# Due times for ScalarE and VectorE work, and a last product in two column pieces

## The chip, the cores and the metric

The kernel runs on one core of a Trainium2 chip. Its time is what the device takes for one execution, in microseconds (us), and the median over several executions is compared. The engines are named as in the profile: PE (TensorE, matrix products), ACT (ScalarE), DVE (VectorE), POOL (GpSimd) and SP (SyncE). PE writes its results to PSUM, from where ACT and DVE read them. In this kernel POOL and SP mostly issue DMAs.

## What is computed

An attention without softmax feeds a two-layer network. There are 8 batches, 12 heads, 448 positions and a head size of 64; the network has width 768 and 2048 inner units, and runs over all 8 x 448 = 3584 rows.

```python
scores = scale * np.matmul(q, k.transpose(0, 1, 3, 2))   # scale = 1/sqrt(64)
attn = np.maximum(scores, 0.0) ** 2 / S                  # S = 448
attn_out = np.matmul(attn, v)
x = attn_out.transpose(0, 2, 1, 3).reshape(B * S, H * D) # 3584 x 768
h = x @ w_in                                             # 768 x 2048
g = 0.5 * h * (1.0 + erf(h / sqrt(2)))
out = g @ w_out                                          # 2048 x 768
```

## The kernel before, in words

**Stages of one batch.** The heads of a batch b are taken four at a time, in three groups g. For each group there are seven *score steps* i of 64 keys (`add_steps`, 539). A step is four matmuls into a PSUM tile `ps` (L552), then a relu with scaling into `a_sq`, either on ACT (L564) or on DVE (L566), then a square on DVE (L573). After the seven steps of a group comes the product *AV* (`add_av`, 600; L614) into a PSUM tile `pav`, and two copies of it into `xT`, one for each half, on DVE (L316) or ACT (L318). Then the first layer (`add_f1`, 650): sixteen products `psh` with the input weights, six matmuls each (L661), and after each a Gelu on ACT (L671) into the ring `h_sb`.

**The second layer.** It works on groups of two times 128 rows (`add_group`, 732). Each group is a matrix product by quarters with seven products of eight matmuls of 384 columns (L768) instead of eight, made from sums of inputs (`s_sb`, four *sums* on DVE, L749) and sums of weights (`t_sb`, made once, L706). The results leave PSUM by *passes* (`passed`): a copy (L316) or an addition (L802) on DVE into `p_sb` or the output tile `osb`. The last product of a group, `p3`, is added onto bank "c" after `c22` has read that bank, and its pass `c12` adds it to the right half of the group's first output tile. Then SP issues the stores (`store_rows`, L729). A store is split in two DMAs where the row order of the output asks for it. In the last group (g = 13) the store of that right half goes by the queues of ACT and SP, one DMA each. The first two blocks of rows are multiplied plainly (`add_plain`, L850).

**Buffers.** PSUM has three `w` tiles of two banks each, which `ps` and `pav` share, and two `f`-pool tiles of one bank, which `psh` and the products of the second layer take from the same pool. There are 14 `a_sq` tiles.

**Transposes.** For batch 0 and 1 PE transposes q and k. From batch 2 on, DVE reorders them into `pk` and `pq` (L395, L406), SP issues seven transposing DMAs into `kT` and `qT` (L498, L507), and POOL, behind a small copy `gate` (L519) that waits for the transposes, issues the loads of the batch after.

**What sets the order.** Everything is written as operations with the engines that may do them, an estimated duration, what they depend on, and which buffers they need and free (`Op`, 86). A planner (`Scheduler`, 100) places them in its own estimated time and so decides, while the program is built, on which engine and in which order each stands; the chip then runs each engine's queue in that order, and waits where a result or buffer is missing. The first 270 operations or so, up to about 57 us, have their engine and order written out in ORDER (68). After that PE follows a fixed list `pe_q`, which interleaves batch b's scores with the first layer of batch b - 1 and groups of the second layer. In each group g the list has two score steps, then the AV of the group before (or a product of the network where there is none), then two score steps, and later the other three. POOL has a fixed list as well. For ACT, DVE and SP, `pick` (131) takes among the next operations the one with the smallest estimated start plus a hand-set bias; the passes have -0.4 us, the sums -0.3, the Gelus -0.57. From batch 2 on, the relu of step i = 1 stands on DVE and all others on ACT (`DVE_STEPS`, 586). The estimates of the planner are no times of the chip.

Of the kernel before, what the change touches and what calls it, by code (L numbers as in the profile page):

```python
# [26 lines left out]
ND = DM // 2  # L27
# [13 lines left out]
ATT1_BIAS = 0.0  # L41
HALF_BIAS = -0.07
GELU_BIAS = -0.57
RELU_DVE = 0.3
DMA_FREE = 4.54
DMA_LAT = 2.13
SWITCH = 0.09
LEAD = 8
DVE_STEPS = (1,)
HALF_M = 6  # L50
PASS_BIAS = -0.4
SUM_BIAS = -0.3
TSUM_BIAS = 0.2
LEADS = {3: 8}
CARRY = 4


def cols(half):
# [9 lines left out]
ORDER = """  # L68
# [31 lines left out]
class Scheduler:  # L100
# [4 lines left out]
    WINDOW = 60  # L105

    def __init__(self, buffers):
        self.free = {"PE": 6.0, "ACT": 2.6, "DVE": 1.0, "POOL": 1.25, "SP": 0.9}
        self.bufs = {name: [0.0] * n for name, n in buffers.items()}
        self.open, self.mode, self.dma = [], None, DMA_FREE  # L110
        self.landed = [0.0] * 8
        self.log = []
    def add(self, engines, fn, deps=(), **kw):
        op = Op(engines, fn, deps, **kw)
        self.open.append(op)
        return op
# [11 lines left out]
            t = max(t, f)  # L128
        return t

    def pick(self, ops):
        top = None
        for n, op in enumerate(ops):
            t = self.ready(op)
            if t is None:
                continue
            for x, (eng, dur, lat) in enumerate(op.engines):
                est = max(t, self.free[eng])
                if isinstance(lat, tuple):
# [32 lines left out]
    def run(self, fixed):  # L172


        fixed = {e: list(v) for e, v in fixed.items()}
        inside = {id(o) for v in fixed.values() for o in v}

        names = {"P": "PE", "A": "ACT", "D": "DVE", "G": "POOL", "S": "SP"}
        gone = set()
        for word in ORDER.split():  # L180
            op, eng = self.open[int(word[1:])], names[word[0]]
            _, dur, lat = next(e for e in op.engines if e[0] == eng)
            self.commit(max(self.ready(op), self.free[eng]), op, eng, dur, lat)
            gone.add(id(op))
        fixed = {e: [o for o in v if id(o) not in gone] for e, v in fixed.items()}
        rest = [o for o in self.open if id(o) not in inside | gone]
        while rest or any(fixed.values()):
# [18 lines left out]
        self.open = []  # L206
        n = len(ORDER.split())
        for est, op, eng in self.log[:n] + sorted(self.log[n:], key=lambda x: x[0]):
            op.fn(eng)


@with_exitstack
def kernel(
# [325 lines left out]
    def add_steps(todo, bias=0.0, dve=False):  # L539
        for blocks in todo:  # L540
            box = {}
            w = S if blocks[0][3] is None else HS
            used = w * len(blocks)

            def fn_qk(e_, blocks=blocks, box=box, w=w):
                ps = box["ps"] = w_pp.tile([128, 2, NB], F32, tag="w", name="ps")
                for x, (b, g, i, half) in enumerate(blocks):
                    qT, kT = get_T(b)
                    for e in range(2):
                        r = slice(64 * e, 64 * e + 64)  # L550
                        for j in range(2):
                            nc.tensor.matmul(  # L552
                                ps[64 * j : 64 * j + 64, e, x * w : x * w + w],
                                kT[r, g, i * 128 + 64 * j : i * 128 + 64 * j + 64],
                                qT[r, 2 * g + j, cols(half)],
                                start=True,
                                stop=True,
                            )

            def fn_relu(e_, box=box, used=used):  # L560
                box["a2"] = apool.tile([128, 2, S], BF16, tag="a", name="a_sq")
                ar, ps = box["a2"][:, :, :used], box["ps"][:, :, :used]
                if e_ == "ACT":
                    A.activation(ar, ps, AF.Relu, scale=c_att)  # L564
                else:
                    V.tensor_scalar(  # L566
                        ar, ps, c_att, 0.0,
                        op0=mybir.AluOpType.mult, op1=mybir.AluOpType.max,
                    )
# [162 lines left out]
    def add_group(g):  # L732
# [30 lines left out]
        def product(bank, left, right, deps, need=(), frees=(), joint=()):  # L763
            def fn(e):
                if need:
                    box[bank] = f_pp.tile([128, NB], F32, tag="f", name="pso")
                for kf in range(K2):
                    nc.tensor.matmul(  # L768
                        box[bank][:, :ND],
                        left()[:, kf],  # L770
                        right[:, kf],
                        start=bool(need) and kf == 0,
                        stop=kf == K2 - 1,
                        skip_group_check=not need,
                    )

            d = K2 * (ND / 2400 + 0.0025)
            o = sch.add(
                (("PE", d, d + 0.24),), fn, deps, need=need, frees=frees, joint=joint, mode="F"
            )  # L780
# [13 lines left out]
                box["p"] = spool.tile([128, ND], F32, tag="p", name="p_sb")  # L794
            return box["p"]

        def passed(bank, out, other, deps, need=(), frees=(), joint=()):
            def fn(e):
                if other is None:
                    copy(e, out(), box[bank][:, :ND])  # L800
                else:
                    V.tensor_add(out(), box[bank][:, :ND], other())  # L802

            eng = e_copy(ND, 1)
# [19 lines left out]
        c22 = passed("c", part(1, right), part(1, right), [v3, p5])  # L824
        p4 = product("b", lambda: h(1, o2), tsum[4], [v3])
        c21 = passed("b", part(1, left), first, [p4, v3], frees=("f", "p"))
        p3 = product("c", lambda: box["s", 4], quad[1, 1], [c22, s4], frees=("s4",))
        c12 = passed("c", part(0, right), part(0, right), [p3], frees=("f",))
        if g < NG - 1:
            sch.add((("SP", 0.6, 2.8),), store(1, full, [nc.sync] * 2), [c22, c21], frees=("osb",))  # L830
            sch.add((("SP", 0.6, 2.8),), store(0, full, [nc.sync] * 2), [c11, c12], frees=("osb",))
# [6 lines left out]
        return [(1.3, o) for o in (p1, p6, p2, p7, p5, p4, p3)]  # L838

    plain = []  # L840

# [238 lines left out]
```

## Time and profile before

| | |
|---|---|
| median of 8 runs | 380.13 us |
| lowest and highest of them | 379.27 and 381.23 us |
| the profiled execution: its time | 379.27 us |
| its span, first to last instruction | 377.5 us |
| busy PE / DVE / ACT / POOL | 365.7 / 246.4 / 201.8 / 45.8 us |
| granted TensorE clock | 1.000 |
| relus on ACT (L564) / on DVE (L566) | 141 of 914 ns / 28 of 1088 ns on average |
| squares on DVE (L573) | 169 of 616 ns |
| DMA | 42.93 MB, 114 GB/s on average |

Lines such as L552 are lines of the kernel's file. In the timeline, each row has the start, the length, the engine with the line and operation, what is written from what, and how many instructions are merged in the row. A bracket at the end says how long the engine had been idle before, and what the work was waiting for. In the view of waits, each row has the engine and line that waited, what it waited for, the total in us, how often, and the longest. A matmul's own length is modelled and longer than its distance to the next one, so distances are read from the starts. "SPq" and "ACTq" rows are DMA issues on the queues of these engines.

### The profile page before, as it was taken

What the parts mean: (1) busy time and instruction counts of PE and PEld (TensorE: products, weight loads), DVE (VectorE), ACT (ScalarE), POOL (GpSimd) and SP (SyncE); (2) the same over time, 40 slices, a digit from 0 to 9 for tenths busy, and PEclk for the clock granted to TensorE, in tenths of its full rate; (3) what the DMA queues carried; (4) which work ended last, traced back from release to release, by engine and by line L of the source; (5) the groups of instructions that cost most, each with busy time, mean ns of one, the idle gap of its engine ahead of it and who ended that gap; (6) DMA issues with size and microseconds to landing.
All of it is one profiled execution on the core that took longest, in us unless ns stands there. A gap on an engine that the chain in (4) does not pass through costs nothing.

```text
span 377.5 us, 7915 instructions
## 1 busy us (share of the span) xinstructions
PE 365.7 (97%) x3333; PEld 201.5 (53%) x3333; DVE 246.4 (65%) x446; ACT 201.8 (53%) x307; POOL 45.8 (12%) x69
## 2 busy tenths in 40 slices
PE   8799999999999989999999999999999999999995
PEld 7576544455544555555555455555554555555663
DVE  3999981599944788843888458745884468601662
ACT  4998865875248635465346775566336762143000
POOL 8666402200020030002000200000000000000000
PEclk9999999999999999999999999999999999999999
DMA  9999999995779979649517590740203002200222
GB/s 172 196 201 205 200 188 112 203 203 107 127 147 177 146 112 224 148 93 159 104 42 158 96 197 2 173 58 3 82 3 85 0 2 84 67 18 2 83 85 83
DMA packets 69523, 42.93 MB, mean 114 GB/s; under 512 B 37744, under 2 KB 66032, under 8 KB 69488
## 3 DMA queue, kind: packets, MB, share of 16 engines
q0 software_dynamic: 30512, 22.47, 39.9%
q1 hardware_dynamic: 38656, 19.46, 24.3%
q8 instruction: 26, 0.43, 0.4%
q10 hardware_dynamic: 320, 0.51, 0.4%
q14 instruction: 9, 0.07, 0.1%
HBM read 45.61 MB, written 11.01 MB: 150 GB/s over the span
## 4 chain that ended last, share of the span: by engine, by line
PE 82%; DVE 7%; DMA 6%; ACT 1%; SPq 1%; POOL 1%; issue 1%; POOLq 0%
PE psh L661 34%; PE pso L768 32%; PE ps L552 8%; PE pav L614 6%; DMA wout_sb<-in_moe_w_out_dram 4%; DVE a_sq L573 2%; DVE a_sq L566 2%; DMA nk<-in_k_dram 1%; PE pso L850 1%; DVE s_sb L749 1%; SPq L507 1%; DVE osb L802 1%; DMA qT<-pq 1%; ACT a_sq L564 1%; DVE xT L316 1%
## 5 line engine op out<-in xcount | busy, mean ns | idle before, releaser
L661 PE MATMUL psh<-xT,win_sb 128*128 128x448 bf16 (+1 forms) x804 | 151.5, 344 | 0.1
L564 ACT ACTIVATE a_sq<-ps 128x896 bf16<-128x896 f32 (+1 forms) x141 | 123.2, 914 | 47.4 <-PE ps L552 47.2
L573 DVE TENSOR_TENSOR a_sq<-a_sq 128x896 bf16<-128x896 bf16 (+1 forms) x169 | 100.6, 616 | 41.8 <-ACT a_sq L564 41.6
L661 PEld LDWEIGHTS <-win_sb 128*128 128x128 bf16 x804 | 76.1, 98 | 71.4 <-issue 9.8
L671 ACT ACTIVATE h_sb<-psh 128x448 bf16<-128x448 f32 x128 | 70.0, 547 | 68.1 <-PE psh L661 56.2
L768 PEld LDWEIGHTS <-s_sb 128*128 128x128 bf16 x416 | 40.0, 98 | 28.3 <-issue 2.5
L552 PE MATMUL ps<-qT,kT 64*64 64x448 bf16 (+1 forms) x756 | 47.9, 336 | 4.6 <-DVE a_sq L566 1.8
L566 DVE TENSOR_SCALAR a_sq<-ps 128x896 bf16<-128x896 f32 x28 | 30.4, 1088 | 22.9 <-PE ps L552 22.5
L768 PEld LDWEIGHTS <-h_sb 128*128 128x128 bf16 x312 | 29.8, 98 | 22.1 <-issue 2.8
L768 PE MATMUL pso<-t_sb,s_sb 128*128 128x384 bf16 x208 | 38.1, 326 | 0.0
L768 PE MATMUL pso<-wout_sb,h_sb 128*128 128x384 bf16 x208 | 38.1, 326 | 0.0
L768 PE MATMUL pso<-wout_sb,s_sb 128*128 128x384 bf16 x208 | 38.0, 326 | 0.0
L614 PE MATMUL pav<-a_sq,v_sb 64*64 64x448 bf16 (+1 forms) x756 | 37.0, 330 | 0.8 <-ACT a_sq L564 0.4
L552 PEld LDWEIGHTS <-kT 64*64 64x64 bf16 x756 | 18.6, 105 | 27.5 <-issue 22.3
L802 DVE TENSOR_TENSOR osb<-pso,p_sb 128x384 f32<-128x384 f32 x39 | 21.7, 557 | 12.7 <-PE pso L768 10.5
L614 PEld LDWEIGHTS <-v_sb 64*64 64x64 bf16 x756 | 21.2, 107 | 13.2 <-issue 2.5
L318 ACT CAST xT<-pav 128x448 bf16<-128x448 f32 (+1 forms) x25 | 12.4, 495 | 22.4 <-DVE xT L316 13.3
L316 DVE COPY p_sb<-pso 128x384 f32<-128x384 f32 x13 | 7.2, 557 | 23.4 <-PE pso L768 22.9
L519 POOL COPY gate<-qT 128x4 bf16<-128x4 bf16 x5 | 1.0, 207 | 154.7 <-DMA qT<-pq 154.7
L316 DVE CAST xT<-pav 128x448 bf16<-128x448 f32 (+1 forms) x29 | 16.3, 566 | 5.1 <-ACT xT L318 4.3
L768 PE MATMUL pso<-t_sb,h_sb 128*128 128x384 bf16 x104 | 19.0, 326 | 0.0
L802 DVE TENSOR_TENSOR osb<-pso,osb 128x384 f32<-128x384 f32 x26 | 14.5, 557 | 5.4 <-PE pso L768 2.9
(42 smaller groups left out, 165.2 us busy)
## 6 DMA issues: line engine op xcount, KB each, us to landing
nk<-in_k_dram POOLq DMA_DIRECT2D x5, 672.0 KB, 6.5
nq<-in_q_dram POOLq DMA_DIRECT2D x5, 672.0 KB, 11.8
v_sb<-in_v_dram POOLq DMA_DIRECT2D x5, 672.0 KB, 14.6
out_dram<-osb SPq DMA_DIRECT2D x8, 336.0 KB, 2.8
wout_sb<-in_moe_w_out_dram POOLq DMA_DIRECT2D x2, 1152.0 KB, 11.6
v_sb<-in_v_dram POOLq DMA_DIRECT2D x9, 224.0 KB, 8.7
out_dram<-osb SPq DMA_DIRECT2D x7, 288.0 KB, 2.9
out_dram<-osb SPq DMA_DIRECT2D x8, 240.0 KB, 3.0
```

The costliest lines, as they stand in the source:

```text
L316: V.tensor_copy(dst, src)
L318: A.copy(dst, src)
L507: nc.sync.dma_start_transpose(get_T(b)[0][:, :, bass.ts(c, KC)], get_p()[0][:, c, :])
L552: nc.tensor.matmul(ps[64 * j : 64 * j + 64, e, x * w : x * w + w], kT[r, g, i * 128 + 64 * j : i * 128 + 64 * j + 64], qT[r, 2 * g + j, co ...
L564: A.activation(ar, ps, AF.Relu, scale=c_att)
L566: V.tensor_scalar(ar, ps, c_att, 0.0, op0=mybir.AluOpType.mult, op1=mybir.AluOpType.max,)
L573: V.tensor_mul(box["a2"][:, :, :used], ar, ar)
L614: nc.tensor.matmul(pav[0][o2 : o2 + 64, e, :w], vt[b][r, 2 * g + e, bass.ts(i, D)], box["a2"][r, e, o : o + w], start=(i == 0), stop=(i == ...
L661: nc.tensor.matmul(ph[:, x * n : x * n + n], win_sb[:, kd, bass.ts(m + x, 128)], xT[b][:, kd, c], start=(kd == 0), stop=(kd == KD - 1),)
L671: A.activation(h_ring()[:, m : m + nm, o + c.start : o + c.stop], box[0][:, :S].rearrange("p (x n) -> p x n", x=nm), AF.Gelu,)
L768: nc.tensor.matmul(box[bank][:, :ND], left()[:, kf], right[:, kf], start=bool(need) and kf == 0, stop=kf == K2 - 1, skip_group_check=not need,
L802: V.tensor_add(out(), box[bank][:, :ND], other())
```

## The change

`run` now places all operations twice. After each placing, `deadlines` computes for every operation a latest start. It lays the PE operations of the plan end to end, without gaps, with the last of them where the plan has it, and works back from there: an operation has to start early enough for everything that depends on it, or that takes a buffer it frees, to start at its own latest time. Operations which nothing depends on may come 50 us after their place in the plan. In the second placing, for ACT and DVE, `pick` looks only at the engine's own possibilities and takes, of all operations that can start within `NEAR` = 0.5 us of the earliest, the one with the earliest latest start; the hand-set biases don't count there. From batch 2 on, each relu may go to either engine. `RELU_DVE`, the handicap of DVE for it, is 0.8 us instead of 0.3. The operations that ORDER lists keep engine and order.

In the last group, the last product `p3` becomes two products, of the columns 0 to 255 and 256 to 383, with a pass and a store of its own for each.

```diff
-RELU_DVE = 0.3
+RELU_DVE = 0.8
...
-DVE_STEPS = (1,)
...
+LAST = 256
+PASSES = 2
+NEAR = 0.5
...
-    def pick(self, ops):
-        top = None
+    def pick(self, ops, only=None):
+        top, near = None, []
...
             for x, (eng, dur, lat) in enumerate(op.engines):
+                if self.late and only not in (None, eng):
+                    continue
...
                 key = (est + op.bias + x * op.other, n)
                 if top is None or key < top[0]:
                     top = (key, est, op, eng, dur, lat)
+                near.append((est + x * op.other, est, n, op, eng, dur, lat))
+        if top and self.late and only in ("ACT", "DVE"):
+            edge = min(near)[0] + NEAR
+            top = min(
+                ((self.late[id(o)], n), est, o, eng, dur, lat)
+                for at, est, n, o, eng, dur, lat in near if at <= edge
+            )
         return top
...
     def run(self, fixed):
+        for _ in range(PASSES):
+            self.reset()
+            self.place(fixed)
+            self.deadlines()
+        self.open = []
+        n = len(ORDER.split())
+        for est, op, eng in self.log[:n] + sorted(self.log[n:], key=lambda x: x[0]):
+            op.fn(eng)
+
+    def deadlines(self):
+        after = {id(o): [] for o in self.open}
+        for o in self.open:
+            for d in o.deps:
+                if id(d) in after:
+                    after[id(d)].append(o)
+                elif isinstance(getattr(d, "op", None), Op):
+                    after[id(d.op)].append(o)
...
+        for name, v in given.items():
+            n = self.buffers[name]
+            for x, o in enumerate(v):
+                if x + n < len(takers[name]):
+                    for y in [o] + list(o.joint):
+                        after[id(y)].append(takers[name][x + n])
...
+        pe = [o for _, o, e in order if e == "PE"]
+        ideal, at = {}, 0.0
+        for o in pe:
+            ideal[id(o)] = at
+            at += o.engines[0][1]
+        shift = pe[-1].start - ideal[id(pe[-1])]
+        for est, o, e in reversed(order):
+            t = ideal[id(o)] + shift if e == "PE" else est + 50.0
+            for s in after[id(o)]:
+                if id(s) in self.late:
+                    t = min(t, self.late[id(s)] - (o.done - o.start))
+            self.late[id(o)] = t
...
-            tops = [self.pick(v) for v in by.values()]
+            tops = [self.pick(v, e) for e, v in by.items()]
...
-            if dve is True:
+            if dve:
                 eng += (("DVE", d, d + 0.12),)
-            elif dve and blocks[0][2] in DVE_STEPS:
-                eng = (("DVE", d, d + 0.12),)
...
-                        box[bank][:, :ND],
+                        box[bank][:, n0:n1],
                         left()[:, kf],
-                        right[:, kf],
+                        right[:, kf, n0:n1],
...
-                    V.tensor_add(out(), box[bank][:, :ND], other())
+                    V.tensor_add(
+                        out()[:, n0:n1], box[bank][:, n0:n1], other()[:, n0:n1]
+                    )
...
-        p3 = product("c", lambda: box["s", 4], quad[1, 1], [c22, s4], frees=("s4",))
-        c12 = passed("c", part(0, right), part(0, right), [p3], frees=("f",))
+        ends = [(0, ND)] if g < NG - 1 else [(0, LAST), (LAST, ND)]
+        p3 = [
+            product("c", lambda: box["s", 4], quad[1, 1], [c22, s4], n0=n0, n1=n1)
+            for n0, n1 in ends
+        ]
+        p3[-1].frees = ("s4",)
+        c12 = [
+            passed("c", part(0, right), part(0, right), [o], n0=n0, n1=n1)
+            for o, (n0, n1) in zip(p3, ends)
+        ]
+        c12[-1].frees = ("f",)
...
-            sch.add((("SP", 0.6, 2.8),), store(0, right, [nc.scalar, nc.sync]), [c12])
+            for o, (n0, n1) in zip(c12, ends):
+                c = slice(ND + n0, ND + n1)
+                sch.add((("SP", 0.6, 2.8),), store(0, c, [nc.scalar, nc.sync]), [o])
...
-        add_steps(steps(b), dve=1)
+        add_steps(steps(b), dve=True)
```

More of the change, by code (lines that the diff above doesn't have):

```diff
@@ L107, in __init__, with reset @@
     def __init__(self, buffers):
+        self.buffers = buffers
+        self.open = []
+        self.late = {}
+        self.reset()
+    def reset(self):
         self.free = {"PE": 6.0, "ACT": 2.6, "DVE": 1.0, "POOL": 1.25, "SP": 0.9}
-        self.bufs = {name: [0.0] * n for name, n in buffers.items()}
-        self.open, self.mode, self.dma = [], None, DMA_FREE
+        self.bufs = {name: [0.0] * n for name, n in self.buffers.items()}
+        self.mode, self.dma = None, DMA_FREE
         self.landed = [0.0] * 8
         self.log = []
+        for op in self.open:
+            op.start = op.done = None
     def add(self, engines, fn, deps=(), **kw):
@@ L172, in run, with place @@
     def run(self, fixed):
+        for _ in range(PASSES):
+            self.reset()
+            self.place(fixed)
+            self.deadlines()
+        self.open = []
+        n = len(ORDER.split())
[9 more added lines that the diff above has]
+                    after[id(d.op)].append(o)
+        takers = {}
+        for _, o, _ in self.log:
+            for name in o.need:
+                takers.setdefault(name, []).append(o)
+        given = {}
+        for _, o, _ in self.log:
+            for name in o.frees:
+                given.setdefault(name, []).append(o)
+        for name, v in given.items():
[4 more added lines that the diff above has]
+                        after[id(y)].append(takers[name][x + n])
+        self.late = {}
+        t = math.inf
+        order = sorted(self.log, key=lambda x: x[0])
+        pe = [o for _, o, e in order if e == "PE"]
[10 more added lines that the diff above has]
+            self.late[id(o)] = t
+    def place(self, fixed):
         fixed = {e: list(v) for e, v in fixed.items()}
@@ L205, in run @@
                 rest.remove(op)
[L206 to L209, printed above, removed]
 @with_exitstack
@@ L761, in add_group, with product @@
         s4 = sum_op(4, sub, lambda: h(1, o1), lambda: box["s", 2], done + [s2])
-        def product(bank, left, right, deps, need=(), frees=(), joint=()):
+        def product(bank, left, right, deps, need=(), frees=(), joint=(), n0=0, n1=ND):
             def fn(e):
@@ L775, in fn @@
                     )
-            d = K2 * (ND / 2400 + 0.0025)
+            d = K2 * ((n1 - n0) / 2400 + 0.0025)
             o = sch.add(
@@ L795, in first, with passed @@
             return box["p"]
-        def passed(bank, out, other, deps, need=(), frees=(), joint=()):
+        def passed(bank, out, other, deps, need=(), frees=(), joint=(), n0=0, n1=ND):
             def fn(e):
@@ L801, in fn @@
                 else:
-                    V.tensor_add(out(), box[bank][:, :ND], other())
-            eng = e_copy(ND, 1)
+                    V.tensor_add(
+                        out()[:, n0:n1], box[bank][:, n0:n1], other()[:, n0:n1]
+                    )
+            eng = e_copy(n1 - n0, 1)
             return sch.add(
@@ L826, in add_group @@
         c21 = passed("b", part(1, left), first, [p4, v3], frees=("f", "p"))
-        p3 = product("c", lambda: box["s", 4], quad[1, 1], [c22, s4], frees=("s4",))
-        c12 = passed("c", part(0, right), part(0, right), [p3], frees=("f",))
+        ends = [(0, ND)] if g < NG - 1 else [(0, LAST), (LAST, ND)]
[9 more added lines that the diff above has]
+        c12[-1].frees = ("f",)
         if g < NG - 1:
             sch.add((("SP", 0.6, 2.8),), store(1, full, [nc.sync] * 2), [c22, c21], frees=("osb",))
-            sch.add((("SP", 0.6, 2.8),), store(0, full, [nc.sync] * 2), [c11, c12], frees=("osb",))
+            sch.add((("SP", 0.6, 2.8),), store(0, full, [nc.sync] * 2), [c11] + c12, frees=("osb",))
         else:
@@ L834, in add_group @@
             sch.add((("SP", 0.6, 2.8),), store(1, full, [nc.sync] * 2), [c22, c21])
-            sch.add((("SP", 0.6, 2.8),), store(0, right, [nc.scalar, nc.sync]), [c12])
+            for o, (n0, n1) in zip(c12, ends):
+                c = slice(ND + n0, ND + n1)
+                sch.add((("SP", 0.6, 2.8),), store(0, c, [nc.scalar, nc.sync]), [o])
         for bb in bs:
             readers.setdefault(bb, []).extend(mine)
-        return [(1.3, o) for o in (p1, p6, p2, p7, p5, p4, p3)]
+        return [(1.3, o) for o in (p1, p6, p2, p7, p5, p4)] + [(1.3 / len(p3), o) for o in p3]
     plain = []
```

## The prediction, made before the changed kernel ran

> **What bounds the kernel now.** I read the page's busy shares first, then the whole list of waits for PE, then PE's timeline with the idle time before each piece.
>
> ```profile
> PE 365.7 (97%) x3333; PEld 201.5 (53%) x3333; DVE 246.4 (65%) x446; ACT 201.8 (53%) x307; POOL 45.8 (12%) x69
> ```
>
> PE is busy for 365.7 of 377.5 us and its sequence is the same after the change but for the last product, so only its 11.8 idle microseconds can be won. Part of them lies in the first 24 us, whose order is written out in ORDER (68) and stays; 4.2 us lie behind the last product. In between, from 57 us on, PE's timeline shows idle time only here:
>
> ```profile
> 87.19 0.38 PE L552 MATMUL ps<-qT,kT 64*64 64x448 bf16 x4 [0.52 <-DVE a_sq L566]
> 137.54 0.38 PE L552 MATMUL ps<-qT,kT 64*64 64x448 bf16 x4 [1.11 <-DVE xT L316]
> 149.21 0.38 PE L552 MATMUL ps<-qT,kT 64*64 64x448 bf16 x4 [0.56 <-DVE a_sq L566]
> 195.32 0.38 PE L552 MATMUL ps<-qT,kT 64*64 64x448 bf16 x4 [0.23 <-DVE a_sq L566]
> 232.33 0.38 PE L552 MATMUL ps<-qT,kT 64*64 64x448 bf16 x4 [0.23 <-DVE a_sq L566]
> ```
>
> The view of waits counts five under DVE a_sq with 1.8 us; the fifth, 0.23, stands at 278.45. The sum is 0.52 + 1.11 + 0.56 + 3 x 0.23 = **2.88 us**. All six are one place in the program: two score steps (QK0, QK1), the product AV, two more score steps (QK2, QK3). The scores have three PSUM buffers; AV takes the third, so QK3 waits until QK1's relu, which line 586 forces onto VectorE, or AV's two copies have given one back. The timeline shows why it is late at 195:
>
> ```profile
> 193.11 0.56 DVE L802 TENSOR_TENSOR osb<-pso,p_sb 128x384 f32<-128x384 f32 x1 [0.21 <-PE pso L768]
> 193.44 0.92 ACT L564 ACTIVATE a_sq<-ps 128x896 bf16<-128x896 f32 x1 [3.46 <-PE ps L552]
> 193.59 0.68 DVE L749 TENSOR_TENSOR s_sb<-h_sb 128x1024 bf16<-128x1024 bf16 x1
> 194.18 1.08 DVE L566 TENSOR_SCALAR a_sq<-ps 128x896 bf16<-128x896 f32 x1
> 194.95 0.53 ACT L318 CAST xT<-pav 128x448 bf16<-128x448 f32 x1 [0.60 <-PE pav L614]
> ```
>
> A pass and a sum stand ahead of the relu on DVE, while ACT is free for 0.6 us. PE wanted QK3 at 195.09; the relu ended at 195.26.
>
> **Part 1, deadlines.** Nothing is removed from PE, and each relu, square, sum, pass and copy is still done once. From batch 2 on (18 such places) the relu may go to either engine, and each of the two engines takes, among what can start within 0.5 us (NEAR), what the PE sequence needs first. DVE's relu carries 0.8 (RELU_DVE) against that 0.5, so DVE takes it only when it has nothing else to start within about 0.3 us.
>
> At the six places DVE has a sum, a subtraction or squares at hand, so I expect QK1's relu on ACT, right behind QK0's. Three relus in a row last 2.54 us on ACT (187.44), one 0.92, so their pitch is (2.54 - 0.92) / 2 = 0.81 us. At 193.44 that puts QK1's relu at 194.25 to 195.17, QK3 at about 195.23 with the 0.06 us that the row shows from relu to QK3: a wait of 0.14 for 0.23. By the same count, from the start of QK0's relu on ACT (85.07, 134.78, 146.99) and the time at which PE was ready (86.67, 136.43, 148.65), the others keep 0.19, 0.14 and 0.13. Together 0.19 + 0.14 + 0.13 + 3 x 0.14 = 0.88 us stay and **2.0 us go**. What is late next is QK1's relu still, now on ACT. If DVE took the relu ahead of the sum, at 193.59, it would end at 194.67 and the waits would vanish: the other end is 2.88. AV's copies that ACT does at 194.95 then wait for the relu or go to DVE; their next reader, the batch's first product by the input weights, starts at 199.55, which hides it; without that cover it would cost the 0.6 us of a copy.
>
> At the other places DVE takes the relu now without a wait on PE: beside products of the input weights (L661) DVE was idle before it for 0.47, 0.72, 0.78 and 2.99 us (121.96, 206.74, 218.93, 247.16), and at 178.82, 261.95 and 308.06 its next work is a square, ready only when ACT's relu ends 0.75 us later. By the rule of the change these stay on DVE, at no cost. Relus that go to ACT take about 1.0 us each from DVE. ACT carries 0.92 each for it; in the dense stretches of DVE (80 to 100, 130 to 160) ACT is busy 3.3 to 7.1 of 10 us, which covers it.
>
> The planner's order is not in this trace, so its ends stay open: 2.88 us won, or the loss of rival 2. DMA issues: transposes and loads are the same in number. SP and POOL are moved only by what releases them (rival 1).
>
> **Part 2, the last product in two pieces.** Last rows of before:
>
> ```profile
> 371.77 1.46 PE L768 MATMUL pso<-wout_sb,s_sb 128*128 128x384 bf16 x8
> 372.55 1.62 SPq L729 DMA_DIRECT2D out_dram<-osb  x3
> 373.27 0.56 DVE L802 TENSOR_TENSOR osb<-pso,osb 128x384 f32<-128x384 f32 x1 [0.74 <-PE pso L768]
> 373.86 0.38 ACTq L729 DMA_DIRECT2D out_dram<-osb  x1
> ```
>
> Added: 8 matmuls with weight loads, one add, two DMA issues. A matmul of 384 columns has a pitch of 162.6 ns (27.31 us for 168 in the chain). The 256-column piece takes 8 x 108 = 0.87 us. A 128-column matmul with its load costs between 54 ns (a third of 162.6) and 107 ns (the 45 spins of L916 start from 1.0 to 5.7 us). The nearest row in the running kernel is the transposes with 128 columns, 14 in 0.51 us, two of which fill the width of one: 73 ns, so 0.58 us, and PE ends 0.15 later (0 to 0.42). Adds: 384 columns take 0.557 us and 448-column copies 0.624, so 0.157 + n/960: 0.42 for 256 and 0.29 for 128, with a pitch of 0.09 us less than that when back to back (0.47 for 0.56).
>
> If the first add runs beside the second piece's matmuls, the last add ends 0.27 us earlier. SP's queue is free at 373.33 (its first two issues last 0.78), issues piece 1 until about 373.70, then piece 2: 0.15 earlier than 373.85. If the first add has to wait for the second piece, the adds end at 373.27 + 0.34 + 0.29 = 373.90, 0.07 later, and SP's last issue comes at about 374.06, 0.21 later. The last transfer shrinks from 144 to 48 KB: by 0.7 us (the rows near the end land in 2.3 and 1.6) or by nothing (ACT's 48 KB took 2.5). So the tail is -0.85 to +0.63 us in all; In every row of before the passes out of a bank follow the last product into it and never run beside one, so I take the second case, with half of the transfer's gain: +0.21 + 0.15 - 0.35, **0.0**.
>
> The Trainium skill (PSUM — Partial Sum Buffer, "PSUM bank collisions raise a hardware error") speaks against this part: two engines may not touch one bank in one group of 32 partitions at once, even at disjoint columns. Both pieces lie in bank "c"; no run here shows two engines in one bank. By this rule the add must be held back, which is the sum of +0.21; without it the sum has -0.15.
>
> **Sum.** The profiled execution took 379.27 us, 1.77 more than its span of 377.5. -2.0 + 0.0 makes it 377.3. The median of the runs shown is 380.13, 0.86 above the profiled one, so I forecast **378.1**.
>
> **Rivals.** *1. Batch 3's transposes come late.* The copies pk and pq on DVE feed seven transposes on SP. A deadline counts one transpose's latency, not SP's queue of seven (97.77 to 107.93), so it looks some 7 us looser than it is. For: the gate that follows the last one is at 109.51, batch 3's first scores at 110.24, a slack of 0.73. If a copy of AV (0.55), two passes (0.94) and two sums (1.24) go ahead of pk at 97.32, scores come 2.73 - 0.73 = 2.0 us late and eat the gain: 380.1. Against: the relu at 86.05 leaves DVE, which starts pk up to 1.0 us earlier, and all else before 97.32 is due anyway. The other batches have 11 us or more.
>
> *2. ACT takes the relus at the quiet places too, and the time ends above before.* Beside L661 products ACT does a Gelu of 0.54 first: at 206.11 it would start QK0's relu at 206.72, QK1's at 207.53, and end at 208.45, where PE wants QK3 at 208.03 (L552 at 207.84, 0.19 a step): 0.48 us. Seven such places make 3.4, the three at 178, 262 and 308 another 0.4, the six 0.9: 4.7 against 2.88, **+1.8 us, 381.9**. It decides from six quiet places on (2.9 of new waits against the 2.0 won). For: copies or squares waiting on DVE would shut its relus out. Against: the idle times above.
>
> *3. The planner's clock is not the chip's.* Its 0.5 us look-ahead may idle an engine, and as many new waits of 0.1 to 0.3 us may come as go, in passes or Gelus: about 379.8, which would also be the result if the order hardly changed.
>
> **Chances.** Forecast 0.55 (376.9 to 379.2), rival 1 0.15, rival 2 0.15, rival 3 0.15. A measurement here can tell about 0.2%, 0.76 us. Faster by more: 0.55 and half of rival 3, 0.62; slower: rival 2 and a little, 0.16; within: 0.22. The range is 376.8 to 380.8: the forecast's own, from all waits gone and a little of the tail, up through rivals 1 and 3; rival 2 and both tail ends together are the 2 in 10 left out.
>
> **What will show it.** Right: the waits of PE L552 for DVE fall from 2.9 to under 0.5 us, with up to 0.9 for ACT a_sq in place; L566 still stands beside L661 products; batch 3's first scores don't wait; the last two adds, 128x256 and 128x128, stand back to back behind the last matmul. Wrong: PE idle before L552 at quiet places with ACT as releaser (rival 2), a wait for a qT transpose near 110 us (rival 1), or waits in L768 and L661, which have none now (rival 3).

## The result, and the profile after

The changed kernel takes **378.37 us** (median of 15 runs, 377.20 to 379.26), the kernel before 379.99 (40 runs in all). The ratio is 0.9955, with a 95% interval of 0.9945 to 0.9965: 1.6 us are won. The profiled execution of the changed kernel took 378.59 us with a span of 376.8, so it lies 0.2 above its median, while that of before lay below its own. The first line of the page says that PE's share is as before, and that DVE has more to do, not less:

```profile
PE 366.3 (97%) x3341; PEld 202.0 (54%) x3341; DVE 250.8 (67%) x448; ACT 199.3 (53%) x306; POOL 45.8 (12%) x69
```

PE's timeline of the changed kernel, with all idle time from 57 us on:

```profile
77.84 0.38 PE L620 MATMUL ps<-qT,kT 64*64 64x448 bf16 x4 [0.43 <-DVE a_sq L634]
87.66 0.38 PE L620 MATMUL ps<-qT,kT 64*64 64x448 bf16 x4 [0.18 <-ACT a_sq L632]
110.92 0.57 PE L620 MATMUL ps<-qT,kT 64*64 64x448 bf16 x8 [0.44 <-issue]
124.33 0.38 PE L620 MATMUL ps<-qT,kT 64*64 64x448 bf16 x4 [0.23 <-ACT a_sq L632]
207.46 0.38 PE L620 MATMUL ps<-qT,kT 64*64 64x448 bf16 x4 [0.32 <-ACT a_sq L632]
```

Of the six places of before, five no longer show idle time and the one at 87 shows 0.18. But four new ones are there. And the shown idle time is too small: a matmul's end is modelled, and covers the beginning of a wait. PE issues the same products in the same order in both kernels, up to the last one, so the starts can be set against each other product by product. That gives the ledger on which the rest of this text builds. It shows by how much PE's start moves at each place (us, negative is won), for the changed kernel's first profile and for a second one, run `changed_again` below:

| place, us | idle shown before | idle shown after | moved, first profile | moved, second profile |
|---|---|---|---|---|
| 77 | | 0.43 | +0.66 | +0.09 |
| 87 | 0.52 | 0.18 | -0.33 | -0.34 |
| 97 and 101 | | | -0.28 | -0.28 |
| 110 | | 0.44 | +0.51 | +0.15 |
| 123 | | 0.23 | +0.40 | +0.40 |
| 137 | 1.11 | | -0.98 | -0.98 |
| 149 | 0.56 | | -0.73 | -0.73 |
| 195 | 0.23 | | -0.40 | -0.40 |
| 207 | | 0.32 | +0.48 | +0.48 |
| 212 and 288 | | | +0.27 | +0.27 |
| 232 | 0.23 | | -0.40 | -0.40 |
| 278 | 0.23 | | -0.11 | -0.11 |
| sum | 2.88 | 1.60 | -0.91 | -1.85 |

An idle time of 0.23 in the view thus stands for 0.40 of PE's time (195, 232 and 123). The change wins 3.23 us: 2.95 at the six places, and 0.28 at 97 and 101, where no view of before shows a wait and where the cause stays open. It gives 1.15 back at 123, 207, 212 and 288, and between 0.2 and 1.2 more at 77 and 110, which differ from one execution to the next. The ledger begins at 57 us and sets single executions against each other, so its sums need not be the 1.6 us between the medians.

At 193 the timeline of the changed kernel answers to the five rows of before:

```profile
192.48 0.56 DVE L868 TENSOR_TENSOR osb<-pso,p_sb 128x384 f32<-128x384 f32 x1 [0.74 <-PE pso L834]
192.81 0.92 ACT L632 ACTIVATE a_sq<-ps 128x896 bf16<-128x896 f32 x1 [3.46 <-PE ps L620]
193.00 1.09 DVE L634 TENSOR_SCALAR a_sq<-ps 128x896 bf16<-128x896 f32 x1
194.32 0.62 DVE L384 CAST xT<-pav 128x448 bf16<-128x448 f32 x1 [0.23 <-PE pav L680]
```

The sum that stood between the pass and the relu is not there; the relu follows the pass at once, still on DVE, and both score buffers are back at 194.1, and PE starts QK3 at 194.29 without a wait. The tail, last rows of the changed kernel:

```profile
370.94 1.48 PE L834 MATMUL pso<-wout_sb,s_sb 128*128 128x256 bf16 x16
371.73 1.98 SPq L795 DMA_DIRECT2D out_dram<-osb  x4
372.46 0.62 DVE L868 TENSOR_TENSOR osb<-pso,osb 128x256 f32<-128x256 f32 x2 [0.76 <-PE pso L834]
372.92 0.86 ACTq L795 DMA_DIRECT2D out_dram<-osb  x2
```

Both adds start behind the sixteenth matmul, 1.52 us after the first one's start, as one add did before at 1.50. From the start of the last product to the end of the span it takes 376.81 - 370.94 = 5.87 us; before, it was 377.51 - 371.77 = 5.74. (These are spans to 0.01 us, as the trace has them; the views show 0.1, and the expectations below work with 5.86 and 5.73.)

### The profile page after: what moved, and what is told of

The parts are those of the page before. It is cut to its first block, busy times and chain, and to the rows that moved or that the text cites. A ratio compares the mean times of both kernels' runs of the same rounds, so it can differ in the third digit from the quotient of the medians.

```text
span 376.8 us, 7922 instructions
## 1 busy us (share of the span) xinstructions
PE 366.3 (97%) x3341; PEld 202.0 (54%) x3341; DVE 250.8 (67%) x448; ACT 199.3 (53%) x306; POOL 45.8 (12%) x69
## 4 chain that ended last, share of the span: by engine, by line
PE 84%; DMA 7%; ACT 2%; DVE 1%; issue 1%; POOL 1%; SPq 1%; DVEq 0%; POOLq 0%; ACTq 0%
PE psh L727 35%; PE pso L834 32%; PE ps L620 8%; PE pav L680 6%; PE pso L929 3%; DMA wout_sb<-in_moe_w_out_dram 2%; DMA nk<-in_k_dram 2%; DMA v_sb<-in_v_dram 2%; ACT a_sq L632 2%; SPq L575 1%; DMA qT<-pq 1%; DVE a_sq L634 1%; ACT h_sb L737 0%; DVE a_sq L641 0%; POOL nk L418 0%
## 5 line engine op out<-in xcount | busy, mean ns | idle before, releaser
L632 ACT ACTIVATE a_sq<-ps 128x896 bf16<-128x896 f32 (+1 forms) x133 | 114.5, 914 | 43.9 <-PE ps L620 43.9
L641 DVE TENSOR_TENSOR a_sq<-a_sq 128x896 bf16<-128x896 bf16 (+1 forms) x169 | 99.4, 617 | 10.4 <-ACT a_sq L632 9.3
L634 DVE TENSOR_SCALAR a_sq<-ps 128x896 bf16<-128x896 f32 x36 | 39.1, 1090 | 40.1 <-PE ps L620 39.7
L834 PE MATMUL pso<-wout_sb,s_sb 128*128 128x384 bf16 (+2 forms) x216 | 38.1, 320 | 0.0
L384 DVE COPY p_sb<-pso 128x384 f32<-128x384 f32 x9 | 5.0, 557 | 26.1 <-PE pso L834 25.8
L868 DVE TENSOR_TENSOR osb<-pso,osb 128x384 f32<-128x384 f32 (+2 forms) x27 | 14.6, 542 | 5.4 <-PE pso L834 3.3
L815 DVE TENSOR_TENSOR s_sb<-h_sb 128x1024 bf16<-128x1024 bf16 x26 | 17.7, 682 | 0.0
```

Of the source, the lines that this page charges most:

```text
L634: V.tensor_scalar(ar, ps, c_att, 0.0, op0=mybir.AluOpType.mult, op1=mybir.AluOpType.max,)
L815: V.tensor_tensor(box["s", n], a(), b(), op=op)
L834: nc.tensor.matmul(box[bank][:, n0:n1], left()[:, kf], right[:, kf, n0:n1], start=bool(need) and kf == 0, stop=kf == K2 - 1, skip_group_ch ...
L868: V.tensor_add(out()[:, n0:n1], box[bank][:, n0:n1], other()[:, n0:n1])
```

## Experiments

The theory: the deadlines win by what they put first on DVE; the split of the last product is no gain, since its first add is held back; the new waits come from two sources, a handicap that shuts relus out of DVE, and queues that stand still behind an instruction which waits for a DMA. The main rivals: the free choice of engine brings the gain, not the deadlines; the split brings part of it. All edits are to the changed kernel, and each ratio is to the kernel before on the same chip.

### one_piece: the last product whole again

```diff
-        ends = [(0, ND)] if g < NG - 1 else [(0, LAST), (LAST, ND)]
+        ends = [(0, ND)]
```

> The changed kernel with its last product whole again (384 columns, one add, two DMAs). Theory (the split is no gain, because the first add is held until the second piece's matmuls end): the wait of the last add after the product's start is 1.50 us again, one add of 0.56 us follows, and from the start of the last product to the end of the span it takes 5.73 us as in before, against 5.86 with the split; time 378.2 us, 0.1 below the changed kernel, which the times alone can't tell. Rival (the split hides most of an add and shortens the last transfer, and is a good part of the gain): 6.0 to 6.4 us from the last product to the end, time 378.7 to 379.0.

377.64 us, ratio 0.9948 (0.9933 to 0.9962). The tail:

```profile
370.01 1.46 PE L834 MATMUL pso<-wout_sb,s_sb 128*128 128x384 bf16 x8
371.51 0.56 DVE L868 TENSOR_TENSOR osb<-pso,osb 128x384 f32<-128x384 f32 x1 [0.74 <-PE pso L834]
```

The tail is 5.73 us, as in before. In all profiles of these experiments the whole product has 5.70 to 5.74 (five), two pieces in one bank 5.84 to 5.87 (six). The split costs 0.10 to 0.17 us and wins nothing; the whole gain comes from the first part of the change. The time is 0.6 below the expected one. Unlooked for, this profile has no idle time shown at 77 and 110, though every engine's order there is that of the changed kernel.

### relu_pinned: deadlines without the choice of engine

```diff
-            if dve:
+            if dve is True:
                 eng += (("DVE", d, d + 0.12),)
+            elif dve and blocks[0][2] == 1:
+                eng = (("DVE", d, d + 0.12),)
...
-        add_steps(steps(b), dve=True)
+        add_steps(steps(b), dve=1)
```

> The changed kernel, but from batch 2 on the relu of score step 1 can only go to DVE and all others only to ACT, as in before; the deadlines stay. Theory (the order on DVE is the cause, deadlines put the relu ahead of sums and passes): of before's six waits of PE the four at 149, 195, 232 and 278 us vanish, those at 87 and 137 stay in part, and 124 and 207 have none, since DVE has the relu there; waits of PE after 57 us sum up to 0.7 to 1.9 us, time 378.0 to 379.0. Rival (the free choice of the engine brings the gain): the four waits of 0.2 to 0.6 us stay, sum near 2.9, time near 380.0.

377.86 us, ratio 0.9951 (0.9933 to 0.9969). PE's idle time after 57 us is in two places, in sum 1.98, a little above what was expected; at 87 it has not shrunk but grown:

```profile
87.50 0.38 PE L620 MATMUL ps<-qT,kT 64*64 64x448 bf16 x4 [1.02 <-ACT a_sq L632]
137.46 0.38 PE L620 MATMUL ps<-qT,kT 64*64 64x448 bf16 x4 [0.96 <-DVE a_sq L634]
```

The four waits at 149, 195, 232 and 278 are gone with the relu on DVE as in before: by the order alone. In the ledger against before they are -0.73 and three times -0.40, and there is nothing to pay at 123, 207, 212 and 288. The free choice is worth something at 87 and 137 only: against the run with one piece those two cost 0.84 and 0.83 more. But the choice costs 0.40, 0.49, 0.15, 0.30 and 0.12 at 123, 207, 212, 278 and 288. The sums, 1.67 and 1.46, nearly cancel, and the times of the two kernels can't be told apart: with the handicap of 0.8, the order alone brings as much as the order and the choice together.

### no_deadlines: the choice of engine without deadlines

```diff
-PASSES = 2
+PASSES = 1
```

> The changed kernel with one placing only, so no deadlines: relus may go to either engine with the handicap of 0.8 us, and the hand-set biases set the order on ACT and DVE. Theory (deadlines bring the gain): the relus that the handicap sends to ACT stand behind Gelus, whose bias of -0.57 puts them first; PE waits at most of the 18 places for ACT a_sq, 0.2 to 0.6 us each, sum 4 to 9 us, time 381.5 to 386. Rival (the free choice alone brings it): sum below 1.9 us, time 378.0 to 379.0.

382.92 us, ratio 1.0081 (1.0066 to 1.0096): slower than before. PE's waits after 57 us:

```profile
PE psh L727 <- ACT h_sb L737: 2.1, 5, 0.5
PE pav L680 <- DVE a_sq L641: 1.0, 2, 0.9
PE ps L620 <- ACT a_sq L632: 0.4, 2, 0.2
```

The time was as expected, the shown waits (3.5 us) were under the 4 to 9 expected, and the mechanism was right only in part. The most time is not lost at QK3 but in the first layer: with 109 relus on ACT (108 in before), PE waits for Gelus that stand behind three relus in a row, for example

```profile
156.66 2.53 ACT L632 ACTIVATE a_sq<-ps 128x896 bf16<-128x896 f32 x3
159.05 1.01 ACT L737 ACTIVATE h_sb<-psh 128x448 bf16<-128x448 f32 x2
159.68 1.67 PE L727 MATMUL psh<-xT,win_sb 128*128 128x448 bf16 x8 [0.49 <-ACT h_sb L737]
```

With that, the two main rivals fall: the gain is there without the split (`one_piece`) and without the choice (`relu_pinned`), and the choice without deadlines loses.

### late_weights: a later estimate for one load

```diff
-            op.done = self.dma + DMA_LAT
+            op.done = self.dma + DMA_LAT + getattr(op, "slip", 0.0)
...
         ld_wout[i] = dma(lambda: load_wout(kf), DM * 128 * WOUTS[i] * 4)
+        ld_wout[i].slip = 2.3 if i == 1 else 0.0
```

> The changed kernel, but the planner counts the second load of the output weights as landing 2.3 us later, so that DVE's first difference of weights that needs it is placed some 3 us later, behind squares and a relu. Theory (the new wait of 0.43 us at 77.84 comes from DVE's queue, which stands still for 3.21 us behind that difference until its DMA lands at 73.2): DVE doesn't stand still there, the wait at 77.84 is gone, the other waits stay, time 0.3 to 0.5 us below the changed kernel, 377.9 to 378.1. Rival (the relu is late there because of its handicap on DVE): the wait of 0.4 stays, time 378.4.

377.60 us, ratio 0.9947 (0.9930 to 0.9965); at 77 there is no wait (-0.12 against before). Against what was expected there is no loss at 110 either, and the time is lower. Since the runs with one piece and of the changed kernel again lose only 0.09 there, this run alone decides nothing. The five profiles with the old estimate and, there, the same order do. DVE's difference of weights (L772 in the changed kernel) waits for the load, and behind it stand a relu and three squares:

```profile
73.22 0.96 DVE L772 TENSOR_TENSOR t_sb<-wout_sb 128x1536 bf16<-128x1536 bf16 x1 [3.21 <-DMA wout_sb<-in_moe_w_out_dram]
74.10 1.08 DVE L634 TENSOR_SCALAR a_sq<-ps 128x896 bf16<-128x896 f32 x1
75.10 1.69 DVE L641 TENSOR_TENSOR a_sq<-a_sq 128x896 bf16<-128x896 bf16 x3
76.70 1.08 DVE L634 TENSOR_SCALAR a_sq<-ps 128x896 bf16<-128x896 f32 x1
```

| start of that difference, us | 72.58 | 72.70 | 72.78 | 73.22 | 73.74 |
|---|---|---|---|---|---|
| run | one_piece | changed_again | queue_aware | the changed kernel | two_banks |
| PE's loss at 77 against before | 0.09 | 0.09 | 0.21 | 0.66 | 1.15 |

Above 72.8 PE loses what the load is late. With the later estimate (here and in `three_repairs`) the loss is gone.

### queue_aware: deadlines that count SP's queue

```diff
+        queue = math.inf
         for est, o, e in reversed(order):
...
+            if e == "SP" and o.engines[0][1] == 1.2:
+                t = queue = min(t, queue - 1.2)
             self.late[id(o)] = t
```

> The changed kernel, but the deadlines count SP's queue: each transposing DMA has to start 1.2 us before the next one in the plan, so that the copies pk and pq that feed seven of them look up to 7 us more urgent. Theory (batch 3's first scores, near 110 us, come late because the deadlines took the transposes for parallel): the copies pk stand ahead of pq, the seven transposes begin at 97 to 98 us instead of 99.3, the gate near 111 comes 0.5 to 1.5 us earlier and PE starts those scores without a wait, 0.2 to 0.4 us earlier against the products before them; all later waits stay; time 377.6 to 378.2. Rival (that wait is only the chance of one execution): gate and scores as in the run with one piece, no difference beyond 0.1 us at this place.

378.18 us, ratio 0.9942 (0.9920 to 0.9964). The gate tells when the transposes have landed:

```profile
106.08 0.19 POOL L590 COPY gate<-qT 128x4 bf16<-128x4 bf16 x1 [37.54 <-DMA qT<-pq]
```

It was at 111.02 in the changed kernel, where the first of them was issued at 99.34 and batch 3's scores waited. Here they begin at 94.34, earlier than expected, and the scores don't wait. But one later wait did not stay as it was; a new one came:

```profile
146.79 0.56 DVE L871 TENSOR_TENSOR osb<-pso,p_sb 128x384 f32<-128x384 f32 x1 [1.86 <-DMA out_dram<-osb]
147.26 1.08 DVE L637 TENSOR_SCALAR a_sq<-ps 128x896 bf16<-128x896 f32 x1
148.40 0.38 PE L623 MATMUL ps<-qT,kT 64*64 64x448 bf16 x4 [0.58 <-DVE a_sq L637]
```

A pass waits until the output tile has been stored, and the relu stands behind it: 0.75 us, more than the 0.22 won at 110 against the run with one piece. It is the same mechanism as at 77 with another DMA. On the other side, the losses at 212 and 288 (0.27) are gone.

### two_banks: the second piece in a PSUM bank of its own

```diff
+        ends = [("c", "f", 0, ND)] if g < NG - 1 else [("c", "f", 0, LAST), ("d", "w", LAST, ND)]
+        p5 = [
+            product(bank, lambda: box["s", 1], tsum[1], [s1, s2], need=(n,), n0=n0, n1=n1)
+            for bank, n, n0, n1 in ends
+        ]
...
+            product(bank, lambda: box["s", 4], quad[1, 1], [x, s4], n0=n0, n1=n1)
+            for x, (bank, n, n0, n1) in zip(c22, ends)
```

> The changed kernel, but the second piece of the last group lies in a PSUM bank of its own: product p5 and its pass are split in the same two pieces, so that p3's pieces are added onto separate banks (8 more matmuls and one more add ahead of the end). Theory (in the changed kernel the first add is held until the second piece's matmuls end because both pieces lie in one bank): the first add starts 1.0 to 1.1 us after the start of the last product instead of 1.52, the last add ends at about 1.8 instead of 2.14, and from the product's start to the end of the span it takes 5.4 to 5.7 us against 5.86. Rival (the add is late for another reason, or can't run beside the matmuls): 1.5 and 5.8 us again.

378.11 us, ratio 0.9947 (0.9928 to 0.9967). The tail:

```profile
371.02 1.04 PE L837 MATMUL pso<-wout_sb,s_sb 128*128 128x256 bf16 x8
371.89 0.61 PE L837 MATMUL psd<-wout_sb,s_sb 128*128 128x128 bf16 x8
372.09 0.42 DVE L872 TENSOR_TENSOR osb<-pso,osb 128x256 f32<-128x256 f32 x1 [0.32 <-PE pso L837]
372.54 0.29 DVE L872 TENSOR_TENSOR osb<-psd,osb 128x128 f32<-128x128 f32 x1
```

The first add now starts 1.07 us after the product's start, beside the second piece's matmuls, and the last ends at 1.81 instead of 2.14. So it was the common place in PSUM that held it back, and the trace shows by what: in the changed kernel only the sixteenth of the last matmuls raises the semaphore for which the first add waits; here the eighth raises it too. The second piece has a PSUM tile of its own here as well as a bank of its own, and no run parts the two. The tail is 5.73, where the whole product has 5.70 to 5.74: of the 0.25 us that the add ends earlier (2.06 before), almost nothing arrives. SP issues the store of the second piece behind that of the first, and so starts its last issue 2.13 us after the product's start, in before 2.09.

### low_handicap: 0.4 us instead of 0.8

```diff
-RELU_DVE = 0.8
+RELU_DVE = 0.4
```

with the edits of `one_piece` and `queue_aware`.

> The changed kernel with the last product whole, the deadlines that count SP's queue, and a handicap for DVE's relu of 0.4 us instead of 0.8, less than the look-ahead of 0.5. Theory (at 123 and 207 both relus stand on ACT behind a Gelu because a copy pq, not urgent, was at hand for DVE and the handicap shut the relu out): L564/L566's successor on DVE has the relu there, those two waits vanish (0.40 and 0.48 us between starts), also the 0.3 near 276 and 288; a wait of some 0.4 may come near 76; in sum 0.7 to 1.3 us below the run with one piece: 376.4 to 377.0. Rival (with relus on DVE its squares and passes come late and as much is lost elsewhere): 377.5 to 378.5.

376.67 us, ratio 0.9904 (0.9882 to 0.9925). Why it wins is seen at 122 us. The changed kernel:

```profile
122.12 0.54 ACT L737 ACTIVATE h_sb<-psh 128x448 bf16<-128x448 f32 x1 [0.59 <-PE psh L727]
122.56 3.34 ACT L632 ACTIVATE a_sq<-ps 128x896 bf16<-128x896 f32 x4
124.33 0.38 PE L620 MATMUL ps<-qT,kT 64*64 64x448 bf16 x4 [0.23 <-ACT a_sq L632]
124.45 0.70 DVE L474 COPY pq<-nq 112x512 bf16<-112x512 bf16 x3 [4.46 <-DMA nq<-in_q_dram]
```

ACT does four relus behind a Gelu, while DVE stands for 4.46 us in front of a copy whose data have not landed. With the low handicap:

```profile
122.14 0.54 ACT L740 ACTIVATE h_sb<-psh 128x448 bf16<-128x448 f32 x1 [0.59 <-PE psh L730]
122.47 1.09 DVE L637 TENSOR_SCALAR a_sq<-ps 128x896 bf16<-128x896 f32 x1 [2.46 <-PE ps L623]
122.66 0.92 ACT L635 ACTIVATE a_sq<-ps 128x896 bf16<-128x896 f32 x1
```

The copy alone is not the reason. With the deadlines of `queue_aware` and the handicap of 0.8 no copy stands there, DVE waits 2.60 us in front of a square, and the relus are on ACT all the same, with the same 0.40 lost:

```profile
121.61 2.53 ACT L635 ACTIVATE a_sq<-ps 128x896 bf16<-128x896 f32 x3
122.55 0.63 DVE L644 TENSOR_TENSOR a_sq<-a_sq 128x896 bf16<-128x896 bf16 x1 [2.60 <-ACT a_sq L635]
```

From batch 2 on DVE has 52 of the 126 relus, 26 in the changed kernel and 18 in before. The ledger against the run with one piece: -0.40 at 123, -0.48 at 207, -0.15 at 212, -0.29 at 278, -0.12 at 288, -0.22 at 110, and +1.00 at 75 to 78, more than the 0.4 expected. Not all of that is the handicap's. What 123, 207 and 278 lose stays in `three_repairs`, which has the handicap of 0.8 with the same deadlines and tail; so those 1.17 us are. The 0.27 at 212 and 288 are won in `queue_aware` as well, with 0.8. At 110 the transposes begin at 98.31, about as late as in the run with one piece (98.70); PE just comes there 1.0 us later.

### three_repairs: queue_aware, late_weights and one_piece together

> The changed kernel with the last product whole, the deadlines that count SP's queue and the later estimate for the second load of output weights; the handicap stays 0.8. Theory: waits at 77 and 110 are gone in every execution, those at 87, 123 and 207 stay, the end is 0.13 us shorter: 377.3 to 377.7, and the spread between executions is smaller than that of the changed kernel (2.1 us), since the two waits that hang on DMAs are gone. Rival (the spread has its origin in the loads of the first 25 us): the same spread.

377.43 us, ratio 0.9926 (0.9903 to 0.9950). The waits at 77 and 110 are gone, the one at 148 has come (0.72). Six runs lie between 377.24 and 378.24; those with one piece, which have neither repair, between 377.32 and 378.59. Where the spread comes from is not settled by that.

### changed_again: the changed kernel once more

> The changed kernel once more, unchanged. Theory (the waits near 77 and 110 us hang on when DMAs land, the others on the order alone): from start to start of PE's products, the places at 87, 123, 137, 149, 195, 207, 232 and 278 show the same times as in the changed kernel's first profile within 0.1 us; the waits at 77 and 110 differ, and the one at 77 goes with the start of DVE's difference of weights (none up to 72.6, 0.2 at 72.8, 0.6 at 73.2, more beyond). Rival (each place varies from one execution to the next): differences of 0.2 us and more at the other places too. Time 378.0 to 378.6.

377.71 us, ratio 0.9939 (0.9919 to 0.9960). The ledger's last column is from this run: the places that hang on the order repeat to 0.01 us, those at 77 and 110 don't. The time is 0.3 below the range expected.

### combined_whole and combined_banks

The edits of `low_handicap` and `late_weights`, and `NEAR = 0.4`; in the second kernel the tail of `two_banks`.

> The kernel of the run with the low handicap (last product whole, queue-aware deadlines, handicap 0.4), with the later estimate for the second load of output weights and a look-ahead of 0.4 us. Theory (the 1.0 us that PE loses there between 75 and 78 comes from DVE standing still behind the difference of weights): that loss goes, 0 to 0.3 us may come near 97, where the plan shows a wait; from the first products after 55 us to the last it takes 0.7 to 1.0 us less than with the low handicap alone, time 375.7 to 376.2. Rival (the order after that stretch changes for the worse): 376.6 or more.

> The same, but with the last product in two pieces in banks of their own instead of whole. Theory: 5.68 us from the last product's start to the end of the span, as in the run with two banks, against 5.7 with the whole product, so no difference that the times can tell: 375.6 to 376.2. Rival (the split in two banks is worth 0.3 us or more): 375.5 or less, and a tail below 5.5.

376.34 us, ratio 0.9905 (0.9887 to 0.9923), and 376.35 us, ratio 0.9904 (0.9885 to 0.9922). Both beat both kernels, and neither can be told from `low_handicap` or from the other. Both times are a little above the range expected, which ends at 376.2. The loss at 75 to 78 is gone as expected (-1.21 against `low_handicap`), but in the first kernel 0.70 of it is given back at 110:

```profile
110.30 0.57 PE L624 MATMUL ps<-qT,kT 64*64 64x448 bf16 x8 [0.63 <-DMA qT<-pq]
```

Its transposes begin no later than in `low_handicap` (98.14 and 98.31), and its gate is at 110.31 for 110.03; but PE now comes 1.3 us earlier to these scores, and finds them late. The second kernel, with the same order there, loses 0.18. From 57 us on the two take 0.47 and 0.99 us less than `low_handicap`, for 0.7 to 1.0 expected. The tails are 5.73 and 5.70 us.

## Why the prediction was right, and where it was not

The forecast of 378.1 us and its sign were right, 378.37 measured. But the sum came out by errors that cancel, so that its closeness is in part luck.

**The waits that go.** 2.0 us forecast, 2.95 found at the six places. Two things were mis-sized. The step "0.52 + 1.11 + 0.56 + 3 x 0.23 = 2.88" took shown idle time for lost time; by starts the same places cost at least 3.2 us, the 2.95 and 0.29 more that `low_handicap` wins at 278. And the step that puts QK1's relu on ACT at all six places was right at 87, 137 and 278 only, where 0.18 is still shown or, at 278, 0.3 of the 0.40 remains. At 149, 195 and 232 DVE took it, without a wait: what I had named as the other end. `relu_pinned` shows that the order on DVE suffices for four of the six.

**"By the rule of the change these stay on DVE, at no cost."** This failed at two of the seven quiet places that it names, 123 and 207, and cost 0.88 us: rival 2, at the price that it named for a place (0.48; measured 0.40 and 0.48) but at two places. I had argued from DVE's idle time in before. That idle time was there, but the handicap of 0.8 shuts the relu out: in the changed kernel copies (pk, pq) stand on DVE there, in `queue_aware` none does at 123, and the loss is the same. With the handicap of 0.4 it is gone. The other 0.27 are lost at 212 and 288 in the first layer, where PE starts right behind a Gelu that ends late on ACT; they vanish with the deadlines of `queue_aware`, and I had not foreseen them.

**"Relus that go to ACT take about 1.0 us each from DVE"** came out the other way in sum: DVE got eight relus more, and is busy for 250.8 us instead of 246.4.

**Rival 1** had the right mechanism, place and cause, SP's queue left out of the deadlines, and too high a price: 0 to 0.51 us for 2.0 (nothing in `two_banks` and `late_weights`). `queue_aware` shows the cause.

**Not foreseen:** the loss at 77. I had looked at what a relu has ahead of it on DVE, and not at what an instruction ahead of it waits for.

**The tail.** 0.0 forecast, +0.13 in the first profile and +0.10 to +0.13 in the others. The second case held: the first add waits for the second piece. The 16 matmuls take 0.02 us more than the 8, for 0.15 forecast, and SP's last issue starts 0.30 later, for 0.36; but the smaller last transfer, for which the sum has -0.35, brought little: from issue to landing it takes 2.48 us on SP, 2.52 before. (Behind the last product lie 4.3 us, not 4.2; nothing rests on that.) The add starts at 1.52 us in a common tile and bank and at 1.07 in separate ones, and it is the program's semaphore that holds it back. The Trainium skill (PSUM — Partial Sum Buffer, "PSUM bank collisions raise a hardware error") states that two engines must be kept out of one bank in one group of 32 partitions. No run here has two engines in one bank at once, so what the chip would do then, none shows.

Still open is why the loads land up to 1.2 us apart (72.58 to 73.74) in executions whose order up to there is the same.

## What to carry to other kernels

Where one engine is never to wait, let the others take first what its sequence needs next; an order by deadlines alone won 2.1 us of PE's time here (`relu_pinned`, by starts from 57 us on), while a free choice of engine without it made the kernel 3.2 us slower (382.92 against 379.74). A choice of engine pays only with a price that lets the idle engine take the work: with a handicap of 0.8 us for DVE's relu, wins and losses nearly cancelled. A deadline has to count queues as well as latencies, and in a queue that runs in order, whatever waits for a DMA belongs behind the urgent work, not ahead of it, by the margin with which the DMA can be late. A product that is split so that its first piece can be read early needs a tile and a bank for each piece, as far as these runs go, and that pays only if the DMA issues behind it don't become the end.

## What the runs showed that I had not expected

A wait of PE that the timeline shows as 0.23 us is 0.40 us from start to start, and one shown as 0.32 is 0.48: the modelled end of a matmul hides some 0.17. In the two pieces of the last product, matmuls of 128x128 weights and 256 columns start 109 ns apart, and those of 128 columns 56 ns apart, each with its own weight load. A third of the 162.6 ns for 384 columns is 54: in these runs of eight, loading the weights hardly shows.
